# Fused retention and mixture of experts on one core: the constants of the attention's beginning loaded as eight rows and spread by TensorE

## The chip, the cores and the metric

The kernel runs on one core of one Trainium2 chip. Its time is the device time of one execution in microseconds (us); smaller is better. Three runs of the kernel before are given by their median, and one further execution was profiled.

## The reference, cut to what matters

Two stages follow each other: a retention attention (causal scores with a decay for each head, no softmax), and a mixture of experts in which every token goes to one of eight experts, with a cap for each expert.

```python
# attention: B, H, S, D = 8, 8, 576, 64
gamma = 1.0 - 2.0 ** (-5.0 - np.arange(H))
rel = pos[:, None] - pos[None, :]
Dmat = np.where(rel >= 0, gamma[:, None, None] ** rel[None], 0.0)
ret = (q @ k.T / 8) * Dmat
x = (ret @ v)                       # to (4608, 512)
...
# mixture: logits = x @ w_gate; tokens are assigned greedily by logit, 576 to an expert
out[mask_e] = np.maximum(x[mask_e] @ w1[e], 0) @ w2[e]
```

The decay of a pair of positions, gamma^(i-j), is written as gamma^i times gamma^-j. The kernel multiplies v by gamma^-j before the products, and the result by 0.125·gamma^i when it leaves PSUM. The second factor is the table of decay powers that this change is about: 8 heads by 576 positions.

## The kernel before, in words

The attention works through 16 units `u`, each of two batches and two heads, so that 128 partitions hold two heads of 64 dimensions. A unit has a first half (`hf` 0) and a second half (`hf` 1). `A(u, hf)` (line 553) makes eight score products on TensorE (PE) and masks them on VectorE (DVE) with `m1`; `A2` (570) does the same for the last 64 positions. `ST(u, c)` (581) accumulates the running state from v and k and copies it with ScalarE (ACT); `across` (594) and `within` (603) add the state's and the block's own part in PSUM; `evict` (620) multiplies by the decay powers `ex` and writes the result to SBUF. `vscale(u, c)` (543) multiplies v by `vs` on ACT.

Every engine takes its instructions in the order in which the code is written. The beginning is lines 748 to 752: two `vscale`, seven matmuls on ones (`warm`), `A(0, 0)`, `ST(0, 0)`; then the loop of line 769 begins with `A(0, 1)`. `A(0, 1)` stands on PE right behind `ST(0, 0)`, and `A(1, 0)` follows after `A2`, `across`, `ST`, `within` and `ST`.

The inputs of a unit are four arrays (k, q, v, and k in rows, called n), 2240 KB in all, loaded with three buffers each. Those of the first two units are cut in two pieces at column 512 and issued by `fetch` (526, 534), in the order of a string: a lower-case letter is a piece of unit 0, a capital one of unit 1, `c` the part of `cst` that holds `vs`, `m1` and `m2`, and `h0`, `h1` the decay powers of two head pairs. All go through SyncE's queue (SP) but the first piece of q, which goes through ACT's. `consts(2)` and `consts(3)` (line 558) load the other two head pairs' powers later. The powers are 128 x 576 values for each of four head pairs, 288 KB each, every row of 64 partitions being the same.

The DMAs of both queues take eight completion semaphores in turn, so that an issue waits until the DMA eight places before it has landed; a wait of that kind shows when that DMA landed. Units from 2 on are loaded whole (`load`, 505), two units ahead of their use (`ahead`, 755).

After the attention come the routing and the eight experts (`moe`, from line 851). The change touches nothing there.

Of the kernel before, what the change touches and what calls it, by code (L numbers as in the profile page):

```python
# [10 lines left out]
F32 = mybir.dt.float32  # L11
# [4 lines left out]
AF = mybir.ActivationFunctionType  # L16
AX = mybir.AxisListType

B, H, S, D = 8, 8, 576, 64
NP, HP, NB = 4, 4, 9  # L20
# [3 lines left out]
CST = HP * 18 + 128 + 64  # L24

def consts_np():
    h = np.arange(H); g = (1.0 - 2.0 ** (-5.0 - h)).astype(np.float64)
    p = np.arange(128)
    at = np.where(np.arange(NB) < 8, 128 * (np.arange(NB) // 2), 512)[None] + np.where(np.arange(NB) < 8, p[:, None], p[:, None] % 64)
    vs = g.reshape(HP, 1, 2)[None] ** -at[:, None, :, None].astype(np.float64)  # L30
    m1 = p[:, None] <= p[None, :]
    m2 = p[:, None] % 64 <= np.arange(64)[None, :]
    ex = 0.125 * g.reshape(HP, 2)[:, p // 64].T[:, :, None] ** np.arange(S)
    f = lambda a: np.ascontiguousarray(a, dtype=np.float32).reshape(128, -1)
    return np.concatenate([f(vs), f(m1), f(m2), f(ex)], axis=1)

def layout(q, k, v):

# [39 lines left out]
class Route:  # L78
# [9 lines left out]
    def fetch(s, nc, fc_d):  # L88
        s.nc = nc
        s.fc = s.pool.tile([128, fc_d.shape[1]], F32, name="rc_f")  # L90
        nc.sync.dma_start(s.fc, fc_d)
# [403 lines left out]
            s.room(cn)  # L495
        yield (2400 if p == 0 else 3500), 0

def attention(tc, nc, P, qk, vk, cst_d, wg_d, rf, xd, Lg):
    cst = P['c'].tile([128, CST + HP*S], F32, name="cst", tag="xg")
    vs = cst[:, 0:HP*18].rearrange("p (h q) -> p h q", h=HP)  # L500
    m1, m2 = cst[:, CST-192:CST-64], cst[:, CST-64:CST]
    ex = cst[:, CST:].rearrange("p (h q) -> p h q", h=HP)
    wg = P['a'].tile([128, HP, 32], F32, name="wg")
    LD = {}
    def load(u, what, cuts=None):
# [10 lines left out]
                nc.sync.dma_start(t, src)  # L516

    pieces = {}
    part = lambda a, b: nc.sync.dma_start(cst[:, a:b], cst_d[:, a:b])

    def consts(hp):
        part(CST + S*hp, CST + S*hp + S)
    load(0, "kqvn", (512,))
    load(1, "kqvn", (512,))

    def fetch(order):
        for x in order.split():
            if x == "c":
                part(0, CST)
            elif x[0] == "h":  # L530
                consts(int(x[1]))
            else:
                (nc.scalar if x == "q0" else nc.sync).dma_start(*pieces[x[0].isupper(), x[0].lower()].pop(0))
    fetch("k0 q0 c v0 n0 k1 q1 h0 v1 n1 K0 Q0 h1 V0 N0 K1 Q1 V1 N1")
    R = Route(P['c'], P['a'], P['ps'], Lg, P['ident'])
    G = 16*NB
    PS, AM, PX, XT = {}, {}, {}, {}
    ident = P['ident']
# [4 lines left out]
    def vscale(u, c):  # L543

        v = LD[u, 'v']
        for h in range(2):
            x = v[:, 256*c:256*c+256].rearrange("p (b h d) -> p h b d", b=2, h=2)[:, h] if c < 4 else v[:, 1024+64*h:1088+64*h]
            nc.scalar.activation(x, x, AF.Copy, scale=vs[:, u % HP, 4*c+h:4*c+h+1])  # L548
# [4 lines left out]
    def A(u, hf):  # L553

        if u == 16: return
        if hf == 0 and 2 <= u + 1 < 16:
            if u < 3:
                consts(u + 1)
            if u == 2:
                R.fetch(nc, rf)  # L560
                nc.sync.dma_start(wg[:, :, 0:8], wg_d.rearrange("(hp p) e -> p hp e", p=128))
        pa = two.tile([128, 2, 4, 128], F32, name="pA", tag="A", bufs=1)
        for j in range(4):
            s = slice(512*hf + 128*j, 512*hf + 128*j + 128)
            for r in range(2):
                nc.tensor.matmul(pa[:, r, j], LD[u, 'k'][half(r), s], LD[u, 'q'][half(r), s], start=True, stop=True, skip_group_check=True)  # L566
        AM[u, hf] = P['w'].tile([128, 2, 4, 128], F32, name="am", bufs=2)
        nc.vector.tensor_tensor(AM[u, hf], pa, m1[:, None, None, :].to_broadcast([128, 2, 4, 128]), op=ALU.mult)  # L568
# [12 lines left out]
    def ST(u, c):  # L581

        if u == 16: return
        if c == 0: PS[u] = PS2[:, 2*(u % 2):2*(u % 2)+2]
        v, n = LD[u, 'v'], LD[u, 'n']
        for b in range(2):
            for h in range(2):
                s = slice(256*c + 128*b + 64*h, 256*c + 128*b + 64*h + 64)
                nc.tensor.matmul(PS[u][half(h ^ b), b], n[:, s], v[:, s], start=(c == 0 and b == 0), stop=False, skip_group_check=True)  # L589
        st = P['w'].tile([128, 2, 64], F32, name="S", bufs=4)  # L590
        nc.scalar.activation(st, PS[u], AF.Copy)
        SI[u, c] = st
# [109 lines left out]
    def at(g, f, *a):  # L702
        fill.setdefault(g, []).append((f, a))

    def rest(it):
        for _ in it:
            pass
    def both(a, b):
        while True:
            x, y = next(a, 0), next(b, 0)  # L710
            if x == y == 0:
                return
            yield
# [3 lines left out]
    first = (0, 4, 9, 13, 18, 22, 27, 31)  # L717
    for bp in range(NP - 1):
        h = [(bp+1)*4*NB + g for g in first]
# [17 lines left out]
    for k, b0 in enumerate((0, 3)):  # L737
        g1 = G - NB + b0 + 3 + (1 if k == 0 else 0)
        c0 = bp*NB + b0
        at(g1, logits, bp, b0, b0+3)  # L740
        at(g1 + (1 if k == 0 else 2), logits2, bp, b0, b0+3)
        it = R.count_first(c0, c0+3)
        if k == 0:
            for i in range(6):
                at(g1+2+i//2, next, it, None)
        else:
            at(G-1, lambda it, k: rest(both(it, R.first_digits(27, 30) if k else iter(()))), it, k)
    vscale(0, 0)
    vscale(0, 1)
    P['warm'](7)  # L750
    A(0, 0)
    ST(0, 0)
    nc.gpsimd.memset(wg, 0.0)

    def ahead(g):
# [56 lines left out]
    c = R.first_digits(30, 36)  # L812
# [247 lines left out]
    run.regs = regs  # L1060
    return run

def build(tc, nc, qk, vk, cst, wg, rf, w1, w2, out):
    with ExitStack() as top:
        P = {}
        P['c'] = top.enter_context(tc.tile_pool(name="c", bufs=1))
        P['ps'] = top.enter_context(tc.tile_pool(name="ps", bufs=1, space=bass.MemoryType.PSUM))
        dr = top.enter_context(tc.tile_pool(name="dr", bufs=1, space=bass.MemoryType.DRAM))
        top.enter_context(tc.manual_schedule())
        xd = dr.tile([N, DM], F32, name="xd")  # L1070
        full = P['c'].tile([128, 512], BF16, name="full")
        nc.vector.memset(full, 1.0)
        it = P['c'].tile([128, 128], I32, name="it")
        nc.gpsimd.iota(it, pattern=[[1, 128]], base=0, channel_multiplier=-1)
        P['ident_r'] = P['c'].tile([128, 128], F32R, name="ident")
        nc.vector.tensor_scalar(P['ident_r'], it, 0.0, None, op0=ALU.is_equal)
        P['ident'] = P['ident_r'].bitcast(F32)
        Lg = P['c'].tile([128, 36, 8], F32, name="Lg")
        mix = Mixer()

        def warm(n):

            ps = P['ps'].tile([128, DM], F32, name="warm", tag="y", bufs=2)
            for _ in range(n):
                nc.tensor.matmul(ps, full[:, :128], full, start=True, stop=True)
        P['warm'] = warm
        banks = ExitStack()

        def open_banks(name):
            P['pb'] = banks.enter_context(tc.tile_pool(name=name, bufs=1, space=bass.MemoryType.PSUM))  # L1090
            return P['pb']

        def bank(tag, shape, name, dt=F32):
            return P['pb' if tag[0] == "h" else 'ps'].tile(shape, dt, name=name, tag=tag, bufs=1 if tag in "tr" else 2)
        P['open'], P['close'], P['bank'] = open_banks, banks.close, bank
        top.callback(banks.close)
        with ExitStack() as ctx:
            Q = dict(P)
            for name, bufs in (("a", 1), ("ld", 2), ("w", 2), ("xt", 2)):
                Q[name] = ctx.enter_context(tc.tile_pool(name="a_" + name, bufs=bufs))  # L1100
            R, rows = attention(tc, nc, Q, qk, vk, cst, wg, rf, xd, Lg)

            def idle(what):

                if what in ("row", "rows"):
                    if rows:
                        rows.pop(0)()
                    else:
                        warm(1)
                    what = 2*(what == "rows")  # L1110
                if what:
                    warm(what)
            R.idle = idle
            run = moe(tc, nc, P, R, xd, w1, w2, out, mix)
            mix.drain(lambda: 0 in run.regs)
            while rows:
                rows.pop(0)()
        P['w'] = top.enter_context(tc.tile_pool(name="w", bufs=1))
        run()
# [18 lines left out]
```

## Time and profile before

| what | us |
|---|---|
| median of 3 runs | 632.98 (632.65, 632.98, 634.96) |
| the profiled execution | 635.15 |
| its span, first to last instruction | 633.4 |
| PE busy in the span | 605.4 (96%) |
| DVE busy | 406.6 (64%) |
| ACT busy | 289.7 (46%) |

A view's rows give the start and the duration of an instruction, or of several alike in a row, in us from the span's start, and in brackets how long the engine had been idle and what ended that. The granted clock is TensorE's, as a share of 2.4 GHz: 1.00 is the upper of its two levels, 0.50 the lower one of 1.2 GHz. A float32 matmul stands in the trace as two MATMUL records, so "x16" are eight products. SPq and ACTq are the queues' issue instructions.

### The profile page before, as it was taken

To read this page: it belongs to the slowest core of one execution; us is meant where nothing else is said; L and a number is where in the kernel's file an instruction comes from. 1 tells how busy PE (TensorE), PEld (TensorE's weight loads), DVE (VectorE), ACT (ScalarE), POOL (GpSimd) and SP (SyncE) were. 2 spreads that over 40 slices of the span, in tenths; PEclk is the share of its full clock that TensorE was granted. 3 is DMA by queue.
4 is the path that set the end of the run, shared out by engine and by line. 5 is a ranking of instruction groups with operands and counts; after the bars stand their busy time and mean duration, and the time that the engine had idled before them with its cause. 6 is when DMAs were issued, how large, how long until landed. Compare 5 with 4: busy or idle time off the path is not lost.

```text
span 633.4 us, 14764 instructions
## 1 busy us (share of the span) xinstructions
PE 605.4 (96%) x5752; PEld 516.5 (82%) x5756; DVE 406.6 (64%) x1504; ACT 289.7 (46%) x584; POOL 141.8 (22%) x189
## 2 busy tenths in 40 slices
PE   6999999998899989999999999999999999999995
PEld 4887887865589769978987998789889889889983
DVE  2687979788778868888986996798683203302300
ACT  3555555542455435452572456146415725733510
POOL 0000000000411261261342233151323224131111
PEclk8999999999999999999999999999999999999999
DMA  8999999913688499796789289559938987792521
GB/s 309 399 400 314 389 346 386 312 48 142 172 201 201 169 234 212 194 220 203 168 233 256 60 242 222 177 123 217 244 123 198 202 256 153 185 271 88 99 63 42
DMA packets 51706, 134.20 MB, mean 212 GB/s; under 512 B 5812, under 2 KB 19764, under 8 KB 51636
## 3 DMA queue, kind: packets, MB, share of 16 engines
q0 software_dynamic: 14960, 51.91, 37.7%
q1 hardware_dynamic: 36532, 81.08, 36.5%
q8 instruction: 45, 0.74, 0.5%
q14 instruction: 25, 0.20, 0.1%
q10 hardware_dynamic: 144, 0.26, 0.1%
HBM read 81.33 MB, written 18.87 MB: 158 GB/s over the span
## 4 chain that ended last, share of the span: by engine, by line
PE 62%; DVE 12%; issue 11%; DMA 8%; POOL 4%; ACT 2%; SPq 1%; POOLq 0%; DVEq 0%; ACTq 0%
PE ph L965 22%; PE py L1004 20%; PE pA L566 5%; PE pX L610 4%; PE pS L589 3%; PE pX L601 2%; POOL xg L917 2%; DMA w2l<-raw 2%; DMA raw<-in_w 2%; PE r L332 1%; PE pT L643 1%; DMA qin<-in_qk 1%; POOL out_y L981 1%; PE pt L932 1%; DMA w1l<-raw 1%
## 5 line engine op out<-in xcount | busy, mean ns | idle before, releaser
L1004 PE MATMUL py<-w2h,hb 128*128 128x512 f32 x576 | 188.2, 399 | 0.0
L965 PE MATMUL ph<-xh,w1h 128*128 128x320 f32 (+1 forms) x512 | 152.1, 301 | 2.2 <-DVE xl L935 1.3
L965 PE MATMUL ph<-xh,w1l 128*128 128x320 f32 (+1 forms) x512 | 149.5, 296 | 0.8 <-DMA w1l<-raw 0.8
L965 PE MATMUL ph<-xl,w1h 128*128 128x320 f32 (+1 forms) x512 | 149.5, 296 | 0.0
L1004 PE MATMUL py<-w2l,hb 128*128 128x512 f32 (+1 forms) x320 | 125.4, 392 | 0.1
L1004 PEld LDWEIGHTS py<-w2h,hb 128*128 128x128 f32 x576 | 104.0, 188 | 20.7
L965 PEld LDWEIGHTS ph<-xh,w1h 128*128 128x128 f32 x512 | 96.2, 189 | 4.0 <-DVE xl L935 1.8
L969 ACT ACTIVATE hb<-ph 128x256 fp32r<-128x256 f32 (+1 forms) x128 | 52.2, 409 | 101.3 <-PE ph L965 101.3
L965 PEld LDWEIGHTS ph<-xh,w1l 128*128 128x128 f32 x512 | 96.3, 189 | 1.1 <-DMA w1l<-raw 1.1
L965 PEld LDWEIGHTS ph<-xl,w1h 128*128 128x128 f32 x512 | 96.4, 190 | 0.6 <-DVE cs L336 0.3
L972 DVE SCALAR_TENSOR_TENSOR hb<-ph,hb 128x256 fp32r<-128x256 f32 (+1 forms) x192 | 58.8, 351 | 55.6 <-ACT hb L969 54.9
L917 POOL DMA_INDIRECT xg<-xd,idx x40 | 41.7, 1043 | 194.4 <-ACT w1h L901 161.3
L1021 ACT ACTIVATE yt<-py 128x512 f32<-128x512 f32 x32 | 19.1, 598 | 106.7 <-PE py L1004 80.1
L1004 PEld LDWEIGHTS py<-w2l,hb 128*128 128x128 f32 (+1 forms) x320 | 56.7, 177 | 13.8 <-DMA w2l<-raw 1.0
L981 POOL DMA_INDIRECT out_y<-yt,idx x40 | 40.9, 1022 | 119.4 <-ACT yt L1021 77.5
L906 POOL DMA_DIRECT2D w2l<-raw x32 | 28.8, 900 | 112.5 <-ACT hb L969 110.6
L1024 DVE TENSOR_TENSOR yt<-yt,py 64x512 f32<-64x512 f32 x8 | 5.4, 679 | 69.9 <-ACT yt L1023 69.8
L548 ACT ACTIVATE vin<-vin,cst 128x128 f32<-128x128 f32 (+1 forms) x160 | 48.2, 379 | 3.5 <-DMA vin<-in_vk 3.5
L568 DVE TENSOR_TENSOR am<-pA,cst 128x1024 f32<-128x1024 f32 x32 | 38.9, 1215 | 14.4 <-PE pA L566 14.2
L566 PEld LDWEIGHTS pA<-qin,kin 64*128 64x128 f32 x512 | 32.9, 196 | 12.0 <-DVE Lg L658 3.1
L566 PE MATMUL pA<-qin,kin 64*128 64x128 f32 x512 | 39.1, 294 | 3.3 <-DMA qin<-in_qk 1.7
L906 POOL DMA_DIRECT2D w1l<-raw x31 | 27.7, 906 | 59.9 <-ACT w1l L905 50.2
(177 smaller groups left out, 864.4 us busy)
## 6 DMA issues: line engine op xcount, KB each, us to landing
raw<-in_w SPq DMA_DIRECT2D x64, 512.0 KB, 4.9
w2l<-raw POOLq DMA_DIRECT2D x32, 512.0 KB, 6.0
w1l<-raw POOLq DMA_DIRECT2D x31, 512.0 KB, 6.8
kin<-in_qk SPq DMA_DIRECT2D x14, 576.0 KB, 7.7
qin<-in_qk SPq DMA_DIRECT2D x14, 576.0 KB, 7.2
vin<-in_vk SPq DMA_DIRECT2D x14, 576.0 KB, 8.0
nin<-in_vk SPq DMA_DIRECT2D x14, 512.0 KB
xd<-xr SPq DMA_DIRECT2D x36, 192.0 KB, 6.8
```

What stands on the lines that cost most here:

```text
L548: nc.scalar.activation(x, x, AF.Copy, scale=vs[:, u % HP, 4*c+h:4*c+h+1])
L566: nc.tensor.matmul(pa[:, r, j], LD[u, 'k'][half(r), s], LD[u, 'q'][half(r), s], start=True, stop=True, skip_group_check=True)
L568: nc.vector.tensor_tensor(AM[u, hf], pa, m1[:, None, None, :].to_broadcast([128, 2, 4, 128]), op=ALU.mult)
L610: nc.tensor.matmul(PX[u, hf][half(h), b, 128*c:128*c+128], v[:, a:a+64], AM[u, hf][:, h ^ b, j], start=False, stop=False, skip_group_check ...
L906: nc.gpsimd.dma_start(lo, raw, accum_op=ALU.add)
L917: nc.gpsimd.indirect_dma_start(out=xg[:n, j, :], out_offset=None, in_=xd[:, :], in_offset=bass.IndirectOffsetOnAxis(ap=found[e][:n, j:j+1] ...
L965: T.matmul(ps, w, x, start=(k == 0), stop=(k == 11))
L969: A.activation(hb[:, f, c], ps, AF.Relu)
L972: V.scalar_tensor_tensor(hb[:, f, to+a:to+b], ps[:, a:b], 0.0, hb[:, f, 256*s+a:256*s+b].bitcast(F32), op0=ALU.max, op1=ALU.subtract)
L981: st = nc.gpsimd.indirect_dma_start(out=out[:, :], out_offset=bass.IndirectOffsetOnAxis(ap=found[e][:n, t:t+1], axis=0), in_=y[:n], in_off ...
L1004: T.matmul(ps[:m], a, w, start=(k == 0), stop=(k == last), skip_group_check=True)
L1021: A.activation(y, ps, AF.Copy)
```

## The change

The decay powers are no longer loaded as 128 rows. A small array `er` has eight rows, one for each head: 4 x 128 columns of zeros and ones that say which head a partition of a head pair belongs to, and the 576 powers. `spread(hp)` multiplies the two on PE, in two products of 288 columns, and DVE copies each product from PSUM to `ex`. `spread(0)` and `spread(1)` stand between `A(0, 0)` and `ST(0, 0)`, `spread(2)` and `spread(3)` between `ST(0, 0)` and the loop. The DMAs of `h0` to `h3` are gone; `cst` is now the small part alone, and it and `er` are issued through ACT's queue. An activation of one column, `first`, stands ahead of the first `vscale`, so that ACT's table load comes before the wait for v.

```diff
-    ex = 0.125 * g.reshape(HP, 2)[:, p // 64].T[:, :, None] ** np.arange(S)
-    return np.concatenate([f(vs), f(m1), f(m2), f(ex)], axis=1)
+    return np.concatenate([f(vs), f(m1), f(m2)], axis=1)
+
+def powers_np():
+    h = np.arange(H); g = (1.0 - 2.0 ** (-5.0 - h)).astype(np.float64)
+    e = 0.125 * g[:, None] ** np.arange(S)
+    one = h[:, None, None] == 2*np.arange(HP)[None, :, None] + (np.arange(128) // 64)[None, None]
+    return np.concatenate([one.reshape(H, HP*128), e], axis=1).astype(np.float32)
...
-    cst = P['c'].tile([128, CST + HP*S], F32, name="cst", tag="xg")
+    cst = P['a'].tile([128, CST], F32, name="cst")
+    er = P['a'].tile([H, HP*128 + S], F32, name="er")
...
-    ex = cst[:, CST:].rearrange("p (h q) -> p h q", h=HP)
+    ex = P['c'].tile([128, HP, S], F32, name="ex", tag="xg")
...
-    part = lambda a, b: nc.sync.dma_start(cst[:, a:b], cst_d[:, a:b])
-
-    def consts(hp):
-        part(CST + S*hp, CST + S*hp + S)
+
+    def spread(hp):
+
+        for a in (0, S//2):
+            pe = P['ps'].tile([128, S//2], F32, name="pe", tag="y", bufs=2)
+            nc.tensor.matmul(pe, er[:, 128*hp:128*hp+128], er[:, HP*128+a:HP*128+a+S//2], start=True, stop=True)
+            nc.vector.tensor_copy(ex[:, hp, a:a+S//2], pe)
...
             if x == "c":
-                part(0, CST)
-            elif x[0] == "h":
-                consts(int(x[1]))
+                nc.scalar.dma_start(cst, cst_d)
+                nc.scalar.dma_start(er, er_d)
...
-    fetch("k0 q0 c v0 n0 k1 q1 h0 v1 n1 K0 Q0 h1 V0 N0 K1 Q1 V1 N1")
+    fetch("k0 q0 c v0 n0 k1 q1 v1 n1 K0 Q0 V0 N0 K1 Q1 V1 N1")
...
-            if u < 3:
-                consts(u + 1)
...
+    nc.scalar.activation(P['a'].tile([128, 1], F32, name="first"), ident[:, 0:1], AF.Copy)
     vscale(0, 0)
     vscale(0, 1)
     P['warm'](7)
     A(0, 0)
+    spread(0)
+    spread(1)
     ST(0, 0)
+    spread(2)
+    spread(3)
```

On PE, at the beginning of the attention, the order before is (L566 is `A`, L589 is `ST`, L577 is `A2`, L601 is `across`):

```order
L1085 MATMUL warm<-full 128x512
L566 MATMUL pA<-qin,kin 128x128 x8
L589 MATMUL pS<-vin,nin 64x64 x4
L566 MATMUL pA<-qin,kin 128x128 x8
L577 MATMUL pAt<-qin,kin 64x64 x4
L601 MATMUL pX<-qin,S 64x128 x4
```

and now (L572 is `A`, L530 the product in `spread`, L595 `ST`), with the engine or the DMA that an instruction waits for:

```order
L1096 MATMUL warm<-full 128x512
L572 MATMUL pA<-qin,kin 128x128 [waits DMAHW1_49,DMAHW0_49]
L572 MATMUL pA<-qin,kin 128x128 x7
L530 MATMUL pe<-er 128x288 [waits DMAHW4_49]
L530 MATMUL pe<-er 128x288 [waits PE_49]
L530 MATMUL pe<-er 128x288 [waits DVE_49] x2
L595 MATMUL pS<-vin,nin 64x64 [waits DMAHW5_49,DMAHW3_49,Activation_49]
L595 MATMUL pS<-vin,nin 64x64 [waits Activation_49]
L595 MATMUL pS<-vin,nin 64x64 x2
L530 MATMUL pe<-er 128x288 [waits DVE_49] x4
L572 MATMUL pA<-qin,kin 128x128 [waits DMAHW7_49,DMAHW6_49,PE_49]
```

Four products stand now on either side of `ST(0, 0)`, and `A(0, 1)` is behind all eight; from the third product on each waits for DVE, which empties the PSUM tile of the product two places before.

On DVE, at the same place, with the mask of `A(0, 0)` first and that of `A(0, 1)` last:

```order
L574 TENSOR_TENSOR am<-pA,cst 128x1024 [waits DMAHW2_49,PE_49]
L531 COPY ex<-pe 128x288 [waits PE_49] x8
L574 TENSOR_TENSOR am<-pA,cst 128x1024 [waits PE_49]
L585 TENSOR_TENSOR amt<-pAt,cst 128x128 [waits PE_49]
L636 TENSOR_TENSOR xT<-pX,ex 128x2x2x128 [waits DVE_49,PE_49]
```

Eight copies are new between two masks that stood side by side.

## Rows read from the trace of the kernel before

**Rows 1.** The page: granted clock and DMA share in 40 equal slices of the span.
```profile
PEclk8999999999999999999999999999999999999999
DMA  8999999913688499796789289559938987792521
```

**Rows 2.** Timeline, 0 to 30 us: start, us, engine, line, instruction, idle before.
```profile
0.77 0.39 SPq L533 DMA_DIRECT2D kin<-in_qk  x1
1.22 0.42 SPq L519 DMA_DIRECT2D cst<-in_cst  x1
...
4.87 1.83 PE L566 MATMUL pA<-qin,kin 64*128 64x128 f32 x16 [0.22 <-DMA qin<-in_qk]
...
5.69 1.02 SPq L533 DMA_DIRECT2D kin<-in_qk  x1
5.75 1.28 ACT L548 ACT_TABLE_LOAD   x1 [5.75 <-DMA vin<-in_vk]
...
6.75 1.23 DVE L568 TENSOR_TENSOR am<-pA,cst 128x1024 f32<-128x1024 f32 x1 [5.24 <-PE pA L566]
...
7.04 1.28 ACT L548 ACTIVATE vin<-vin,cst 128x128 f32<-128x128 f32 x4
...
8.42 0.45 PE L589 MATMUL pS<-vin,nin 128*64 128x64 f32 x8 [1.72 <-ACT vin L548]
...
10.38 2.08 PE L566 MATMUL pA<-qin,kin 64*128 64x128 f32 x16 [1.51 <-DMA qin<-in_qk]
...
15.89 0.69 DVE L630 TENSOR_TENSOR xT<-pX,cst 128x512 f32<-128x512 f32 x1 [1.97 <-PE pX L610]
...
21.79 0.33 SPq L519 DMA_DIRECT2D cst<-in_cst  x1
```

**Rows 3.** The same of a DMA issued at 2.15 us: KB, us from issue to landing.
```profile
nin<-in_vk SPq DMA_DIRECT2D x1, 256.0 KB, 6.1
```

**Rows 4.** The chain that ended last, in order of time: start, us, what.
```profile
3.10 7.15 DMA qin<-in_qk
...
10.38 2.08 PE pA L566 x16
...
16.27 1.24 PE pA L566 x16
...
19.98 1.09 PE pA L566 x16
...
22.06 0.88 PE pX L610 x16
...
23.16 1.09 PE pA L566 x16
...
26.73 1.09 PE pA L566 x16
```

**Rows 5.** Half-microsecond windows: busy us of PE, PEld, DVE, ACT, POOL; clock; DMA share; GB/s.
```profile
3.00:3.50 0.50, 0.50 (x2) 0.15 (x1) 0.00 (x0) 0.00 (x0) 0.00 (x0) 1.00 1.03 401
...
9.00:9.50 0.50, 0.00 (x0) 0.00 (x0) 0.00 (x0) 0.20 (x1) 0.00 (x0) 1.00 0.91 347
9.50:10.00 0.50, 0.00 (x0) 0.00 (x0) 0.00 (x0) 0.00 (x0) 0.00 (x0) 0.72 1.04 404
...
16.00:16.50 0.50, 0.50 (x8) 0.38 (x6) 0.50 (x1) 0.18 (x2) 0.00 (x0) 0.50 1.00 371
16.50:17.00 0.50, 0.50 (x10) 0.50 (x10) 0.08 (x1) 0.50 (x3) 0.00 (x0) 0.96 1.01 360
```

**Rows 6.** The chain that ended last, 0 to 120 us: a product of 384 columns.
```profile
44.35 0.78 PE pT L643 x8
```

**Rows 7.** DVE's groups of instructions, shapes apart: out, in, count, busy us, mean ns.
```profile
L630 DVE TENSOR_TENSOR xT<-pX,cst 128x512 f32<-128x512 f32 x12 | 8.3, 690 | 11.0 <-PE pX L601 7.6 <-PE pX L610 3.4
...
L630 DVE TENSOR_TENSOR xT<-pX,cst 128x128 f32<-128x128 f32 x6 | 1.7, 281 | 0.0
```

More of the change, by code (lines that the diff above doesn't have):

```diff
@@ L496, in leave, with attention @@
         yield (2400 if p == 0 else 3500), 0
-def attention(tc, nc, P, qk, vk, cst_d, wg_d, rf, xd, Lg):
-    cst = P['c'].tile([128, CST + HP*S], F32, name="cst", tag="xg")
+def attention(tc, nc, P, qk, vk, cst_d, er_d, wg_d, rf, xd, Lg):
+    cst = P['a'].tile([128, CST], F32, name="cst")
+    er = P['a'].tile([H, HP*128 + S], F32, name="er")
     vs = cst[:, 0:HP*18].rearrange("p (h q) -> p h q", h=HP)
     m1, m2 = cst[:, CST-192:CST-64], cst[:, CST-64:CST]
-    ex = cst[:, CST:].rearrange("p (h q) -> p h q", h=HP)
+    ex = P['c'].tile([128, HP, S], F32, name="ex", tag="xg")
     wg = P['a'].tile([128, HP, 32], F32, name="wg")
@@ L1061, in moe, with build @@
     return run
-def build(tc, nc, qk, vk, cst, wg, rf, w1, w2, out):
+def build(tc, nc, qk, vk, cst, er, wg, rf, w1, w2, out):
     with ExitStack() as top:
@@ L1100, in build @@
                 Q[name] = ctx.enter_context(tc.tile_pool(name="a_" + name, bufs=bufs))
-            R, rows = attention(tc, nc, Q, qk, vk, cst, wg, rf, xd, Lg)
+            R, rows = attention(tc, nc, Q, qk, vk, cst, er, wg, rf, xd, Lg)
             def idle(what):
@@ L1125 @@
     w2 = np.asarray(moe_w2).reshape(E, 8, 128, DM).transpose(0, 2, 1, 3).reshape(E, 128, 4096)
-    arrays = dict(in_qk=qk, in_vk=vk, in_cst=consts_np(), in_wg=moe_w_gate, in_rf=route_consts(), in_w1=w1, in_w2=w2)
+    arrays = dict(in_qk=qk, in_vk=vk, in_cst=consts_np(), in_er=powers_np(), in_wg=moe_w_gate, in_rf=route_consts(), in_w1=w1, in_w2=w2)
     arrays = {n: np.ascontiguousarray(x) for n, x in arrays.items()}
```

## The prediction

> **What bounds the kernel now.** I began with the page's slices. The granted clock is below 0.9 of its full level in the first slice alone, and the DMA engines are busy for over eight tenths in each of the first eight slices, the attention's whole length [rows 1]. So I looked at the first 30 us. The timeline shows how PE begins: `A(0, 0)` from 4.87 to 6.70, a wait of 1.72, `ST(0, 0)` from 8.42 to 8.87, a wait of 1.51, `A(0, 1)` at 10.38 [rows 2]. The chain of waits has the reason for the last one: a piece of q, issued at 3.10, landed 7.15 us later at 10.25. From there the chain is PE nearly without a break: `A(0, 1)` 10.38, `A(1, 0)` 16.27, `A(1, 1)` 19.98, `A(2, 0)` 23.16, `A(2, 1)` 26.73 [rows 4].
>
> Two of these steps are the same work and don't take the same time. `A(0, 1)` to `A(1, 0)` took 16.27 - 10.38 = 5.89 us, `A(1, 1)` to `A(2, 0)` 23.16 - 19.98 = 3.18. The windows say why: the granted clock leaves 1.00 in the window from 9.5 us, after two waits with 0.45 us of matmuls between them, is 0.50 until 16.5, and is back at 0.96 in the next window [rows 5]. The beginning thus holds two losses: PE's waits, and 5.89 - 3.18 = **2.71 us** for the lower clock behind them. The step after it, 16.27 to 19.98, is 3.71 against 3.57 for 23.16 to 26.73: another 0.14.
>
> **What the change costs and gives, part by part.**
>
> *Loads.* Four DMAs of 288 KB go and one of 8 x 4352 bytes = 34 KB comes. At the 401 GB/s of the full engines [rows 5] the 541 KB less ahead of unit 2's inputs are 1.4 us. They shorten no wait by themselves: the piece of q for which `A(0, 1)` waited has k0, q0, c, v0, n0 and k1 ahead of it in the old order and these and `er` in the new one, so it lands near 10.25 either way. What they give is room later. Unit 2's q landed at about 21.79 (the issue of the last `cst` piece waited for it) [rows 2], and `A(2, 0)` wanted it at 23.16 [rows 4]: 1.4 us to spare. A PE more than 1.4 us ahead would have met that load; now the limit is at about 1.4 + 1.4 = 2.8.
>
> *SP and ACT queues.* SP loses the issue of `cst` at 1.22 (0.42 us) [rows 2]; v0, n0, k1 and q1 are issued that much earlier. With the engines full from 3.0 us on I count nothing for it. ACT now issues three DMAs (0.4 us each, done at about 2.0), loads its table (1.28) and runs `first`; all of that ends near 3.5, long before v0 lands at 5.75 [rows 2]. What is queued behind them on ACT is only `vscale`, so they cost nothing.
>
> *The table load.* It stood between v0's landing at 5.75 and the first `vscale` at 7.04, 1.28 us [rows 2]. `vscale` will end at about 7.05 in place of 8.32. But `ST(0, 0)` needs n0 too, and that was issued at 2.15 and landed 6.1 us later, at 8.25 [rows 3]. So this part alone could bring `ST(0, 0)` forward by some 0.1 us, and with `spread` ahead of it, by nothing.
>
> *One product of `spread`.* No row has a matmul of 288 columns and 8 rows. From above: four products of 384 columns took 0.78 us side by side in strips of the array [rows 6]; were that one product's time, 288 columns cost 0.59. In the middle: eight products of 128 columns, two side by side, took 0.88 [rows 4], so four in a row of 0.22, or 0.50 for 288. From below: `A`'s eight products of 128 columns took 1.09 [rows 4]; if its pairs did not overlap, one is 0.136 and 288 columns are 0.31. I take 0.54, as a product over all columns of the array is nearest to the first two. At the lower clock it doubles.
>
> *One copy.* DVE's 512 columns from PSUM took 690 ns, 128 took 281 [rows 7]: 1.07 ns a column, 0.45 us for 288. Eight are 3.6 us, and they stand ahead of `A(0, 1)`'s mask.
>
> *The new path.* DVE must first do the mask of `A(0, 0)`, 6.75 to 7.98 [rows 2]; its copies come behind it, and only two PSUM tiles exist. With 0.05 to 0.1 us for a hand-over, PE goes: products 1 and 2 from 6.72 to 7.80; 3 waits for the copy that ends at 8.43 and runs 8.50 to 9.04; 4 to 9.58; `ST(0, 0)` to 9.98; 5 and 6 to 11.06; 7 waits for a copy that ends at 11.02 and runs 11.10 to 11.64; 8 from 11.66 to 12.20. So `A(0, 1)` starts at **12.20** in place of 10.38, 1.82 later: eight products are more than the two waits hold. But between 6.3 and 12.2 PE is idle for under 1 us in all, where it was idle for 3.2 before the clock fell, so I expect the clock to stay at 1.00 and the next step to take 3.18. The first `evict` at 15.89 [rows 2] finds `ex` ready at about 12.7.
>
> The sum: + 1.82 (later start) - 2.71 (no lower clock) - 0.14 (next step) = **-1.0 us**, which nothing behind it takes back, as unit 2's load has 2.8 us of room. With 0.31 for a product the same walk ends at 11.25 and the sum is -2.0; with 0.59 at 12.5, and -0.7.
>
> The profiled execution took 635.15, so the sum makes it 634.1. Its time stands 2.17 above the median of the three runs, 632.98. Carried to the median, -1.0 gives **632.0 us**, my forecast. About 0.5% (3.2 us) is what a measurement can tell from no change, so this is no change.
>
> **The rivals.**
>
> *The lower clock is not in every execution (chance 0.22).* The profiled execution holds it, and its time (635.15) is next to one of the three runs, 634.96; the two others are 2.0 to 2.3 below, near to the 2.71 of that stretch. If those two kept the clock, the change has nothing to give back there and only brings the runs together: 634.1 whatever the execution, 1.1 over the median. Against it: PE would then have had to wait for unit 2's load after 1.4 us, which is less than that distance. The Trainium skill, "TensorE: Matmul & The Clock Gate", Part 1, says that the same kernel shows different numbers of matmuls at the lower clock from run to run; by that rule the sum for a median run is +1.1 and not -1.0. One trace can't say whether it holds here.
>
> *The products of `spread` are quick (0.20).* If they take about 0.31 the change gives 2.0, 631.0 us; with the two waits holding all of them, `A(0, 1)` at 10.38 and full clock, it is 2.85, 630.1. That is the most it can give, and not yet 0.5%.
>
> *Slower: the clock falls inside `spread` (0.08).* Eight rows of 128 use little of the array, and PE still pauses at the third product. If the granted clock goes to 0.50 at about 9.6 as before, `ST(0, 0)` ends at 10.4, four products take 1.08 each, and `A(0, 1)` starts at 14.7. If the clock returns at 16.5, `A(1, 0)` comes at 18.8, 2.5 us later than now; if it stays down over the whole step of 5.89, at 20.6, 4.3 later: 635.5 to 637.3. The point that decides is the granted clock between 9.5 and 12 us. For it speaks that the clock did fall there after 0.45 us of matmuls between two waits; against it, that the two waits of 1.72 and 1.51 become one pause of 0.7.
>
> *The small load lands late (0.10).* `er` is third in ACT's queue. PE stands still until it lands, with `ST(0, 0)` and `A(0, 1)` behind it. Bytes speak for about 5.8 us: `cst` had landed by 5.69, when the DMA eight places behind it was issued [rows 2]. From a landing at t on, eight products, `ST` and the hand-overs need about 4.9 us; the gain of 2.85 is used up at t = 10.38 + 2.85 - 4.9 = 8.3. A landing as late as q's, 10.25, makes it 1.9 us slower, 634.9. If `cst` lands after 6.75 it delays the mask and the copies in the same way.
>
> **How the numbers follow.** Forecast 0.40, clock not always lost 0.22, quick products 0.20, late load 0.10, clock falls 0.08. All but the slow half of the last and the best end of the quick case lie within 3.2 us of 632.98. For faster by over 0.5% I give 0.07: the quick case at its best (630.1) together with runs that scatter by 2 us. For slower, 0.05: the clock's fall with its higher price. The remaining 0.88 is no change. The range runs from the quick case less some scatter, 630.3, to the late load, 634.9; it leaves out the clock's fall and the best end of the quick case.
>
> **What would show it.** ACT's table load at about 2 us; `er` landed before 6.7; eight products of about 0.54 us between 6.7 and 12.2, the third and the seventh behind a copy; a granted clock of 1.00 from 7 to 17 us; `A(0, 1)` at about 12.2 and the next step in 3.2. All starts from `A(2, 0)` on 1.0 us earlier than now and the rest of the kernel as before. I am wrong if the clock is at 0.50 in any window from 9.5 to 16.5, if `A(0, 1)` starts before 11 or after 13, or if PE waits for a load at unit 2 or 3.

## The result, and the profile after

The change makes the kernel slower: a median of 638.99 us (four runs, 637.22 to 639.88) against 632.82 (four runs), a ratio of 1.0081 with a 95% interval of 1.0055 to 1.0106. The medians lie 6.2 us apart, and the whole interval is above the 0.5% that the prediction counts as no change; the forecast was 632.0 and no change. The profiled execution took 639.05 with a span of 637.3, 3.90 more than before's.

The page's slices of the changed kernel first, as in [rows 1]: the granted clock is below full in the first slice, and a little in the last, and the DMA engines are as full as they were.

```profile
PEclk7999999999999999999999999999999999999998
DMA  9899999923777589697699289649948886892521
```

The timeline of the changed kernel, 0 to 30 us, answers to [rows 2] (columns as there):

```profile
2.31 1.28 ACT L754 ACT_TABLE_LOAD   x1 [2.31 <-issue]
...
4.74 1.39 PE L572 MATMUL pA<-qin,kin 64*128 64x128 f32 x16
...
6.17 1.22 DVE L574 TENSOR_TENSOR am<-pA,cst 128x1024 f32<-128x1024 f32 x1 [4.67 <-PE pA L572]
...
6.50 2.81 PE L530 MATMUL pe<-er 8*128 8x288 f32 x8 [0.37 <-DMA er<-in_er]
...
9.86 4.20 PE L530 MATMUL pe<-er 8*128 8x288 f32 x8
...
13.14 0.46 DVE L531 COPY ex<-pe 128x288 f32<-128x288 f32 x1 [0.50 <-PE pe L530]
...
14.00 2.08 PE L572 MATMUL pA<-qin,kin 64*128 64x128 f32 x16
...
19.41 1.16 PE L572 MATMUL pA<-qin,kin 64*128 64x128 f32 x16
...
26.15 1.16 PE L572 MATMUL pA<-qin,kin 64*128 64x128 f32 x16
```

PE hardly pauses: `A(0, 0)`, four products of `spread`, `ST(0, 0)`, four products, `A(0, 1)`. But the second four products take 4.20 us where the first four take 2.81 with a wait for the mask among them, and `A(0, 1)` takes 2.08, the next step's `A` 1.16. DVE is not what holds the second four back: it waits 0.50 for each product. The windows of the changed kernel (length, PE busy, clock, DMA share, GB/s), which answer to [rows 5], say why:

```profile
7.00:8.00 1.00, 0.91 (x4) 1.00 1.03 392
8.00:9.00 1.00, 1.00 (x4) 0.83 1.04 369
9.00:10.00 1.00, 1.00 (x10) 0.50 1.04 387
...
18.00:19.00 1.00, 1.00 (x14) 0.55 1.00 406
19.00:20.00 1.00, 1.00 (x24) 1.00 1.07 418
```

The clock falls while the fourth product runs, PE having been busy for over nine tenths since 7 us, and stays at the lower level for 10 us (7 before). The kernel before and the changed one, timelines, PE, at `A(2, 0)` and at the attention's last step:

```profile
23.09 1.16 PE L566 MATMUL pA<-qin,kin 64*128 64x128 f32 x16
...
129.09 1.16 PE L566 MATMUL pA<-qin,kin 64*128 64x128 f32 x16
...
131.51 1.16 PE L572 MATMUL pA<-qin,kin 64*128 64x128 f32 x16
```

`A(2, 0)` comes at 26.15, 3.06 later than before in the same view. At the attention's end 2.42 of that is left. The other 1.5 us of the 3.90 arise in the experts' stage: from the first of the experts' lists to the end are 473.7 us, before 472.2 (worked out from the traces).

### The profile page after: what moved, and what is told of

Same layout as the page of the kernel before. It is cut to its first block, busy times and chain, and to the rows that moved or that the text cites. A ratio compares the mean times of both kernels' runs of the same rounds, so it can differ in the third digit from the quotient of the medians.

```text
span 637.3 us, 14798 instructions
## 1 busy us (share of the span) xinstructions
PE 611.1 (96%) x5768; PEld 518.8 (81%) x5772; DVE 409.7 (64%) x1512; ACT 289.8 (45%) x585; POOL 140.7 (22%) x189
## 4 chain that ended last, share of the span: by engine, by line
PE 65%; DVE 12%; issue 10%; DMA 7%; POOL 2%; ACT 2%; POOLq 0%; SPq 0%; ACTq 0%; DVEq 0%
PE py L1015 23%; PE ph L976 20%; PE pA L572 5%; PE pX L616 4%; PE pS L595 3%; PE pX L607 2%; DMA raw<-in_w 2%; DMA w1l<-raw 2%; PE pt L943 2%; PE pT L649 1%; PE r L337 1%; POOL xg L928 1%; DMA w2l<-raw 1%; DMA out_y<-yt,idx 1%; DVE am L574 1%
## 5 line engine op out<-in xcount | busy, mean ns | idle before, releaser
L597 ACT ACTIVATE S<-pS 128x128 f32<-128x128 f32 x64 | 17.7, 277 | 55.7 <-PE pS L595 54.6
L572 PEld LDWEIGHTS pA<-qin,kin 64*128 64x128 f32 x512 | 32.1, 193 | 11.1 <-DVE Lg L664 3.1
```

## The experiments

All ratios are to the kernel before on the same chip, in one set of runs. The duration of `A(0, 1)` serves as a gauge of the clock: 1.16 us at 2.4 GHz, 2.08 at 1.2. It is better than the column of the granted clock, which reads 1.00 until its first recorded change even where `A` takes 2.08 (the change again, below).

**The kernel before, again** (no edit). Is the lower clock of before's profile there in every execution?

> The kernel before, unchanged, for a second profile of it and for more runs. Theory A (in some executions the clock does not fall at the beginning): the granted clock stays near 1.00 from 9.5 to 16.5 us here, A(1,0) starts at about 13.8 and not at 16.27, and the time is about 2 us under 635.15. Theory B (it falls in every execution of the kernel before): 0.50 in those windows again, A(1,0) at about 16.3, and the runs differ by something later in the kernel.

Measured: 636.79, 1.0005 (0.9988 to 1.0023). The chain of its first 30 us:

```profile
6.50 5.91 DMA cst<-in_cst
...
12.43 8.62 DMA qin<-in_qk
21.05 0.14 issue
21.19 1.16 PE pA L566 x16
```

Its `A(0, 1)` (timeline, PE):

```profile
8.04 1.16 PE L566 MATMUL pA<-qin,kin 64*128 64x128 f32 x16
```

It is not: `A(0, 1)` ran at 8.04 at the upper clock, and `A(2, 0)` waited for unit 2's q, whose issue had waited for a piece of `cst`. The same program reaches `A(2, 0)` at 21.19 or at 23.16.

**The change with 128 rows.** The products keep their columns, but `er` has 128 rows: 8 real ones, zeros against ones in the rest, so that the result is the same. Its load carries 32 of them, four memsets write the others.

```diff
-    er = P['a'].tile([H, HP*128 + S], F32, name="er")
+    er = P['a'].tile([128, HP*128 + S], F32, name="er")
+    nc.gpsimd.memset(er[32:64, 0:HP*128], 0.0)
+    nc.gpsimd.memset(er[64:128, 0:HP*128], 0.0)
+    nc.vector.memset(er[32:64, HP*128:], 1.0)
+    nc.vector.memset(er[64:128, HP*128:], 1.0)
-                nc.scalar.dma_start(er, er_d)
+                nc.scalar.dma_start(er[0:32], er_d)
```

> The changed kernel with the products of spread over 128 rows (120 rows of zeros against ones) at the same columns and the same pauses. Theory 1 (products of eight rows do not hold the clock): the granted clock stays near 1.00 from 8.8 to 18 us, A(0,1) starts at about 11.5 to 12.5 in place of 14.00, A(1,0) at about 15 to 16 in place of 19.41, and the time is some 4 us under that of the change. Theory 2 (PE's pauses at the third and fifth product let it fall): 0.50 in those windows as in the change, A(1,0) near 19.4, same time as the change.

Measured: 638.34, 1.0038 (1.0020 to 1.0056). Timeline, PE:

```profile
7.50 2.51 PE L535 MATMUL pe<-er 128*128 128x288 f32 x8 [1.09 <-DMA er<-in_er]
...
10.33 2.54 PE L535 MATMUL pe<-er 128*128 128x288 f32 x8
12.80 1.16 PE L577 MATMUL pA<-qin,kin 64*128 64x128 f32 x16
...
22.73 1.16 PE L577 MATMUL pA<-qin,kin 64*128 64x128 f32 x16
```

Though `er` landed 1.0 us later and PE stood still for 1.09, both groups of products ran at the upper level, 2.5 us each, and `A(2, 0)` came 3.4 us earlier than with eight rows. Some loss stays: 22.73 is 1.5 behind the 21.19 of the run above on the same chip.

**The queue and the table alone, and fills of 128 rows.** Before, with `cst` through ACT's queue and `first`; and before with `P['warm'](6)` ahead of and behind `ST(0, 0)`, six products of 512 columns whose results nobody uses.

> The kernel before with the constants through ScalarE's queue and the early table load alone; the decay powers still come as 128 rows in their old places, and there is no spread. If the loss of the change is spread's alone, this is no slower than the kernel before: A(0,1) starts at 8.7 to 10.4 and A(1,0) at 14 to 16.3. If the other order of the loads or something in the experts' stage costs (weights of expert 0 landing late, as in the changed kernel's trace), it is 2 us or more slower although A(1,0) is not late.

> The kernel before with six bf16 matmuls of 512 columns and 128 rows in each of the two waits (12 in all, results unused). Theory 1 and theory 2 both: the clock stays near 1.00 from 9.5 to 16.5 us; A(0,1) starts at 10.4, A(1,0) at about 13.6 to 14 in place of 16.27; the gain at A(2,0) is 1.3 to 2.5, since unit 2's q lands near 21.8. If the time does not fall by 1 to 2 us against the kernel before, the lower clock at the beginning is not what the runs differ by.

Measured: 1.0001 (0.9985 to 1.0017) and 0.9986 (0.9968 to 1.0004). The queue and the table cost and give nothing that can be told. The fills kept the clock up; their gain, 1.0 us between the medians, lies within the interval, and unit 2's q was then late (timeline, PE):

```profile
8.27 1.47 PE L1087 MATMUL warm<-full 128*128 128x512 bf16 x6
9.67 1.16 PE L566 MATMUL pA<-qin,kin 64*128 64x128 f32 x16
...
21.59 1.16 PE L566 MATMUL pA<-qin,kin 64*128 64x128 f32 x16 [1.14 <-DMA qin<-in_qk]
```

**The change again; addresses; fills of eight rows.** One theory (P in the expectations) was that the change moves tiles to other addresses, and that this costs the time. It was tried from both sides: the change with `ex` padded so that the tiles behind it lie where they did, and before with an unused tile of 32 bytes a partition. Then the fills over 8 rows in place of 128.

```diff
-    ex = P['c'].tile([128, HP, S], F32, name="ex", tag="xg")
+    ex = P['c'].tile([128, CST + HP*S], F32, name="ex", tag="xg")[:, CST:].rearrange("p (h q) -> p h q", h=HP)
...
+    P['c'].tile([128, 8], F32, name="pad")
...
-                nc.tensor.matmul(ps, full[:, :128], full, start=True, stop=True)
+                nc.tensor.matmul(ps, full[:rows, :128], full[:rows], start=True, stop=True)
```

> The change, unchanged, for a second profile and for more runs beside the kernel before on the same chip. Theory 1 (products of eight rows do not hold the clock): 0.50 again within 9 to 18 us, A(1,0) at 18.5 to 19.5, attention 2 us or more later than before; ratio about 1.006 to 1.010. If it is chance in each execution, the clock can be 1.00 here and A(1,0) near 15.5 to 16.

> The change with the tile of the decay powers padded to the 10272 bytes a partition that the old cst had, so that all tiles of the experts' stage lie at the addresses of the kernel before (in the change they lie 32 bytes lower: raw at 51744 in place of 51776). Theory P (the places of the tiles cost): the time from the last score product of the attention to the end falls from about 505 to 507 us to 503.5 to 505.5, and the median is some 2 us under that of the change. Theory not-P: same median as the change within 1 us.

> The kernel before with one unused tile of 32 bytes a partition behind xg, so that all later tiles lie 32 bytes higher. Nothing else differs. Theory P: some 2 us slower than the kernel before (ratio about 1.003), with the whole loss behind the attention. Theory not-P: ratio within 0.998 to 1.002.

> The kernel with the filled waits again (six bf16 matmuls of 512 columns in each of the two waits of the kernel before), but over 8 rows of 128. Theory 1 (eight rows do not hold the clock): the granted clock falls to 0.50 between 8 and 13 us, unlike in the same kernel with 128 rows; A(1,0) at 15.5 or later; time above that of the kernel before by up to 2 us. Theory 2 (only PE's pauses let the clock fall): 1.00 throughout as with 128 rows, A(1,0) at about 13.8.

Measured: the change again 1.0094 (1.0060 to 1.0128), padded 1.0088 (1.0059 to 1.0117), before shifted 1.0005 (0.9990 to 1.0021). So the addresses are not it. The fills of eight rows: 1.0015 (0.9998 to 1.0033).

The change again, timeline, PE: at half speed from its first `A` on, and `A(2, 0)` is 1.9 us later than in the other profile of the same program.

```profile
4.77 2.08 PE L572 MATMUL pA<-qin,kin 64*128 64x128 f32 x16
6.78 4.20 PE L530 MATMUL pe<-er 8*128 8x288 f32 x8
...
11.53 4.21 PE L530 MATMUL pe<-er 8*128 8x288 f32 x8
15.67 2.08 PE L572 MATMUL pA<-qin,kin 64*128 64x128 f32 x16
...
28.07 1.16 PE L572 MATMUL pA<-qin,kin 64*128 64x128 f32 x16
```

A window of the same profile (columns as above), with the clock's column at 1.00 over products at half speed:

```profile
7.00:8.00 1.00, 1.00 (x3) 1.00 1.01 361
```

Before, shifted, timeline, PE: here too `A(0, 1)` is at half speed, but it starts at 8.39, and `A(2, 0)` still has to wait for q.

```profile
8.39 2.08 PE L567 MATMUL pA<-qin,kin 64*128 64x128 f32 x16
...
21.11 1.16 PE L567 MATMUL pA<-qin,kin 64*128 64x128 f32 x16 [0.15 <-DMA qin<-in_qk]
...
127.28 1.16 PE L567 MATMUL pA<-qin,kin 64*128 64x128 f32 x16
```

The change, padded, timeline, PE:

```profile
26.19 1.16 PE L572 MATMUL pA<-qin,kin 64*128 64x128 f32 x16
...
132.25 1.16 PE L572 MATMUL pA<-qin,kin 64*128 64x128 f32 x16
```

These two, from one set, show the loss best: 5.08 us at `A(2, 0)`, 4.97 at the attention's last step, 5.7 in the spans (637.3 and 631.6). In this pair nearly all of it arises in the first 26 us, and nothing after takes it back.

The fills of eight rows, timeline, PE: the second fill takes 2.74 in place of 1.47.

```profile
5.79 1.46 PE L1087 MATMUL warm<-full 8*128 8x512 bf16 x6
...
8.04 2.74 PE L1087 MATMUL warm<-full 8*128 8x512 bf16 x6
10.71 2.08 PE L566 MATMUL pA<-qin,kin 64*128 64x128 f32 x16
```

**Constants and powers in one tile; the same with 128 rows; half of the powers; fills with the queue.** In the change the experts' first gather no longer waits for ACT, which reads `cst`, since its buffer is now that of `ex` alone; theory G was that this hurts the experts' stage. With `cst` and `ex` in one tile it waits again. The second kernel adds the 128 rows. The third has 128 rows too, but spreads two head pairs alone (one on each side of `ST(0, 0)`) and loads the other two, as before. The fourth is before with the queue, the table and `warm(4)`, `warm(3)`.

```diff
-    cst = P['a'].tile([128, CST], F32, name="cst")
+    both_t = P['c'].tile([128, CST + HP*S], F32, name="cst", tag="xg")
+    cst = both_t[:, 0:CST]
-    ex = P['c'].tile([128, HP, S], F32, name="ex", tag="xg")
+    ex = both_t[:, CST:].rearrange("p (h q) -> p h q", h=HP)
...
+            if u < 3:
+                nc.sync.dma_start(both_t[:, CST+S*(u+1):CST+S*(u+2)], cst_d[:, CST+S*(u+1):CST+S*(u+2)])
...
     spread(0)
-    spread(1)
     ST(0, 0)
-    spread(2)
-    spread(3)
+    spread(1)
```

> The change with cst and the decay powers in one tile again, as in the kernel before, so that the first gather of expert 0's rows, which takes that tile's place, waits for ScalarE again. In the four profiles without that wait the stretch from the first list of rows to the end took 473.0 to 473.7 us (475.9 on a chip where the kernel before took 474.7); with it 472.2 to 472.6 on the same chip. Theory G (the lost wait costs): that stretch is 472.0 to 472.7 here, the second load of w2's last pieces no longer comes 8 us after the first, and the median is 1 to 1.5 us under the change's, near 637.5 to 638. Theory not-G: 473.0 or more, median as the change. The clock: half speed in spread as in the three profiles of the change.

> Both repairs together: the products over 128 rows, and one tile. If theory 1 (clock) and theory G (lost wait) hold all the loss, this is within 0.3% of the kernel before: ratio 0.998 to 1.003, with A(1,0) near 16.0 and the stretch from the first list to the end as before. If the ratio stays at 1.005 or more, a third cause is missing.

> The products over 128 rows and one tile, for head pairs 0 and 1 alone: two products before ST(0,0), two behind it; the powers of head pairs 2 and 3 are loaded as 128 rows by SP at units 1 and 2 as before. By theory 1 the clock stays up, A(0,1) starts at 10 to 10.8, A(1,0) at 13.5 to 14, and with 541 KB less ahead of unit 2's q, A(2,0) at 20 to 21: attention over 1.5 to 2.5 us sooner than in the kernel before, ratio 0.995 to 0.999. If PE is held by loads all the same, 0.999 to 1.002.

> The kernel before with the constants through ScalarE's queue, the early table load, and seven bf16 matmuls of 128 rows in its two waits; powers loaded as 128 rows. The clock stays up; A(0,1) at 8.8 to 9.2, A(1,0) at 12 to 13, but A(2,0) waits for unit 2's q at about 21 to 22, so the gain at the attention's end is no more than that of the filled waits alone: ratio 0.996 to 1.000.

Measured: 1.0131 (1.0111 to 1.0152), 1.0053 (1.0030 to 1.0077), 0.9991 (0.9972 to 1.0010) and 1.0010 (0.9995 to 1.0025). G falls: with the wait back the change is no better. The fills with the queue wait for unit 2's q at `A(2, 0)` as those without do. Between eight rows and 128 in one tile lie 641.96 - 636.14 = 5.8 us, but they don't price the clock at the beginning: the two profiles are 6.3 us apart, 2.4 of it at the attention's last step (132.70 and 130.28) and 3.9 in the experts' stage, where both kernels have the same instructions in the same order. The kernel with 128 rows and one tile had a dip of its own (timeline, PE):

```profile
7.28 3.85 PE L536 MATMUL pe<-er 128*128 128x288 f32 x8 [1.37 <-DVE am L580]
...
11.44 2.54 PE L536 MATMUL pe<-er 128*128 128x288 f32 x8
13.91 1.16 PE L578 MATMUL pA<-qin,kin 64*128 64x128 f32 x16
```

PE had stood still for 1.37 us ahead of the products, and the first four took 3.85; then the clock came back while products ran, the second four took 2.54, and `A(0, 1)` had the full clock. With eight rows, once lost, it did not come back in either group. Half of the spread, with 128 rows (timeline, PE):

```profile
8.98 1.24 PE L537 MATMUL pe<-er 128*128 128x288 f32 x4
10.15 1.16 PE L581 MATMUL pA<-qin,kin 64*128 64x128 f32 x16
...
20.86 1.16 PE L581 MATMUL pA<-qin,kin 64*128 64x128 f32 x16 [0.71 <-DMA qin<-in_qk]
```

`A(0, 1)` follows the four products at 10.15, and `A(2, 0)` waits for q: what they cost is covered.

**A later gather; the fills again; half of the spread with eight rows.** Theory C was that the experts' first gather starts too early in the change and collides with weight loads; a copy of its list and a memset now hold it back. The fills were run again together, and the half spread was given back its eight rows.

```diff
+        if e == 0:
+            nc.gpsimd.tensor_copy(P["c"].tile([128, 5], I32, name="hold"), found[e])
+            nc.gpsimd.memset(xg[:, 0, :], 0.0)
...
-    er = P['a'].tile([128, HP*128 + S], F32, name="er")
+    er = P['a'].tile([H, HP*128 + S], F32, name="er")
```

> The change with about 1 us of work on GpSimd (a copy of the row list, a memset of 512 columns) between the first list of rows and the first gather of expert 0, so that this gather starts as late as in the kernel before. Theory C (in the change the expert's stage starts 1 us sooner after its list, and a weight load then meets an accumulating DMA, so that the last piece of w2 is 2 us late): the stretch from the first list to the end falls from 473.0 to 473.7 to about 472.0 to 472.7, the two loads of w2's last pieces are issued at about 25 and 30 us after the list in place of 23 and 31.5, and the median is about 1 us under the change's. Theory not-C: 473.5 or more, median no better than the change's.

> The filled waits with 128 rows again, for a second profile and beside the same with 8 rows on one chip. Theory 1: granted clock 1.00 from the first rise on, A(1,0) before 15, ratio 0.996 to 1.000 to the kernel before.

> The filled waits with 8 rows again. Theory 1: the clock is at half speed in some of the windows from 8 to 15 us, A(1,0) after 15, and the median is 1 to 3 us above that of the same kernel with 128 rows.

> The half spread (head pairs 0 and 1 by products, 2 and 3 loaded), but over 8 rows in place of 128; all else as in the half spread of 128 rows, which had a ratio of 0.9991 with a granted clock of 1.00 throughout and A(2,0) at 20.9. Theory 1: half speed between 7 and 14 us, A(1,0) 2 to 4 us later, A(2,0) at 22 to 24, ratio 1.001 to 1.005. Theory 2: as with 128 rows.

Measured: 1.0122 (1.0094 to 1.0150), 0.9991 (0.9974 to 1.0009), 1.0018 (1.0000 to 1.0035) and 1.0044 (1.0016 to 1.0072). C falls. The fills of 128 rows and of 8 differ by 634.86 - 632.81 = 2.05 us, in the direction of the first time; the intervals of their ratios overlap by 0.0009. Their profiles differ by 3.9 us in span, 3.7 of it at the attention's last step (127.60 and 131.28). `A(0, 1)` with 128 rows, then with 8 (timelines, PE):

```profile
9.54 1.16 PE L566 MATMUL pA<-qin,kin 64*128 64x128 f32 x16
...
12.75 2.08 PE L566 MATMUL pA<-qin,kin 64*128 64x128 f32 x16
```

Half of the spread with eight rows, timeline, PE:

```profile
7.76 1.51 PE L532 MATMUL pe<-er 8*128 8x288 f32 x4
9.20 2.08 PE L576 MATMUL pA<-qin,kin 64*128 64x128 f32 x16
...
21.94 1.16 PE L576 MATMUL pA<-qin,kin 64*128 64x128 f32 x16
```

`A(0, 1)` starts 0.95 earlier than with 128 rows and is yet 1.1 later at `A(2, 0)`. This kernel's runs scatter from 632.61 to 641.55, so this profile (632.84) is among its best.

Taken together, by the gauge:

| matmuls put ahead of `A(0, 1)` | profiles | `A(0, 1)` at 2.08 us | at 1.16 us |
|---|---|---|---|
| none (before and its variants) | 4 | 2 | 2 |
| over 8 rows (change, fills, half spread) | 8 | 8 | 0 |
| over 128 rows (the same) | 6 | 0 | 6 |

In two of the eight (the change again, the fills again) `A(0, 0)` had run at 2.08 already, ahead of any matmul over 8 rows. These did not bring the clock up: in the change again PE is busy without a break from 5 to 21 us. In the other six it fell in them or right behind them.

The runs that were not profiled agree. The mean granted clock of an execution is 0.995 to 0.998 in all 24 runs of the fills of 128 rows, and 0.991 to 0.994 in 20 of the 24 of the fills of eight. It is 0.984 to 0.990 in 26 of the 28 runs of the change and its variants that spread all four head pairs over eight rows, and 0.993 to 0.998 in the 19 over 128. The column misses a lower clock that is there from the start: the profiled run of the change again reads 0.997.

## Why the prediction was wrong

The step that failed is "so I expect the clock to stay at 1.00 and the next step to take 3.18", with its term of -2.71. It took PE's being busy for enough; the runs show that in this kernel the rows of its matmuls decide too: `A(0, 1)` at half speed in eight of eight profiles with eight rows, in none of six with 128. PE was as busy as predicted (idle for 0.3 of the 5.9 us from 6.3 to 12.2), and the clock fell all the same. The rival "the clock falls inside `spread`" named the mechanism, the place and the argument (eight rows use little of the array), and got 0.08, on the argument that the pauses go. Its price of 2.5 to 4.3 us holds between the two profiled executions (3.06 at `A(2, 0)`, 3.90 in all); between the medians (6.2) it does not: 1.2 to 2.0 us of that are explained under "The starting point", and a part lies in the experts' stage, under "Open".

- **The walk.** `A(0, 1)` at 12.20 became 14.00, as four products ran at the lower clock; the next step became 19.41 - 14.00 = 5.41 in place of 3.18. That is 1.80 and 2.23, together the 4.0 by which `A(2, 0)` missed its place (22.1 by the walk). With the clock held, the walk was near: with 128 rows, from a landing 1.0 later, `A(0, 1)` came at 12.80.
- **The sizes.** DVE's copies, by the trace of the changed kernel (ns, least, median, most), are the 0.45 taken; of a product only the two records can be read. Two products at the upper clock take 1.2 us over eight rows (1.23, the first pair of the half spread) and over 128 (1.21), so about 0.6 each where 0.54 was taken; four take 2.5, at the lower clock 4.2.

```profile
L531 DVE COPY ex<-pe x8: 447/457/458, 7.3 to 14.1; 128x288 f32<-128x288 f32 x8
```

- **The starting point.** The rival "the lower clock is not in every execution" is true as well, and it was not a rival but a second error in the same sum: three other profiles of before and its variants without extra matmuls have `A(2, 0)` at 21.11 to 21.93, 1.2 to 2.0 ahead of the profiled 23.09, two without half speed in `A(0, 1)` and one with it (8.39, above). The sum's gain was not there to be had in these three. Nor was it in the runs, as far as their granted clock tells: its mean over a run of before goes from 0.990 to 0.998, and in the four sets the median of those at 0.996 or more is from 0.9 us lower to 0.2 higher than that of the rest, where 2.71 was counted. Carrying -1.0 from the one profile to the median of 632.98 had no ground. The Trainium skill, "TensorE: Matmul & The Clock Gate", Part 1, says that one kernel shows different counts of matmuls at the lower clock from run to run; the traces agree, with `A(0, 1)` at 2.08 and 1.16 us in two profiles of before, and `A(0, 0)` at 1.39 and 2.08 in two of the change.
- **"It lands near 10.25 either way."** It did not: the DMA issued eight places behind that piece of q went out at 8.67, so it had landed by then, and `A(0, 1)` had its data over 5 us before it ran. In the kernel before `A(0, 1)` ran as early as 8.04. The wait that was to hide the second four products was mostly absent, so eight products take time even at full clock: with 128 rows `A(2, 0)` came 1.5 later than before on that chip. The ratios of 1.0038 and 1.0053 hold more than that: of the 1.7 us between the profiles of those two kernels, 0.5 is left at the attention's last step and 1.2 arises in the experts' stage.
- **Right.** The table load ran at 2.31 and `er` was there at 6.49 (before 6.7 was asked); the queue and the table by themselves changed nothing (1.0001); the third product waited for a copy that stood behind the mask. The limit by unit 2's q is there too: in seven profiles it is what `A(2, 0)` waits for, so a quicker beginning gives nothing.
- **Open.** The experts' stage of the change was 1.5 us longer in the first pair of profiles and 0.7 in the pair of padded and shifted kernels. In the seven profiles with the full spread it took 472.3 to 477.2 us (476.2 with one tile, 477.2 with the later gather, 475.9 with 128 rows, 472.3 with both), in the eleven others 470.5 to 474.7. From the first list on all run the same instructions in the same order on each engine, but for the two that hold the later gather back. It shows most where PE waits for the routing's `G` from DVE, in the changed kernel and in the one before (waits from 125 us on: total, times, longest):

```profile
PE r L337 <- DVE G L168: 5.8, 8, 2.0
...
PE r L332 <- DVE G L163: 3.8, 7, 1.1
```

With the full spread this wait is 5.0 to 6.8 us in total, without it 3.5 to 3.9 in eight profiles and 4.9 to 5.3 in three. With one tile and with the later gather, the two slowest, PE stood still there for over 2 us, and the clock was at 0.50 for over 3 us right behind it. With one tile (timeline, PE):

```profile
209.66 0.39 PE L337 MATMUL r<-oh,G 128*128 128x32 bf16 x9 [2.44 <-DVE G L168]
```

So a part of these two kernels' loss is a second dip of the clock, far behind the products. Why DVE comes later there is not shown: neither addresses, the lost wait for ACT nor an early gather explains it, and the ratio of 1.0053 with 128 rows and one tile is, by what was expected of that kernel, the sign of a further cause. Why the clock depends on the rows is not shown either, only that it does here.

No version beat the kernel before by more than the measurement can tell: the best, fills of 128 rows (0.9986 and 0.9991) and half of the spread with 128 rows (0.9991), have 1 in their intervals.

## What to carry to other kernels

Matmuls that are to fill a wait, or to save a load, are worth their price only at the clock at which they run: look at the duration of the work right behind them, and if it doubled, try the same columns over all 128 rows. Before a wait is counted as gained or as cover, look for it in more than one execution, since one profile of a beginning like this may hold a loss that the median run does not have.

## What was not expected of the hardware

- Matmuls over 8 rows did not hold the clock: busy for over nine tenths from 7 us on, PE lost it between 8 and 9 and ran 10 us at 1.2 GHz. Over 128 rows, the same columns kept or regained it, though the 120 rows added to `er` only hold zeros against ones.
- The granted clock's column can read 1.00 over matmuls at half speed, until its first change in the trace: `A(0, 0)` and `A(0, 1)` of 2.08 us in the change's second profile.
- The median of one and the same kernel, before, differed from one set of runs to the next by up to 3.3 us: 632.82, 633.16, 633.28, 633.42 and 636.07. Medians are compared within a set only.
